# Overlap columns of the input-gradient tile copied by ScalarE in two instructions instead of four by GpSimd, its zeros written by VectorE, and the whole order planned anew

## The chip, the cores and the metric

The kernel runs on one core of a Trainium2 chip. It is timed in microseconds of the device, for one execution; the time of a kernel is the median of its runs. The core has five engines that each work through a list of their own: TensorE (PE in the profile; its weight loads are shown as PEld), VectorE (DVE), ScalarE (ACT), GpSimd (POOL) and SyncE (SP), which here does nothing but issue DMA transfers.

## What is computed

A 1-D convolution along time with 31 taps and stride 2, from 256 to 256 channels, then a normalisation of each channel over time, a scale and a shift, and the tanh form of GELU; and the gradients of all of it.

```python
B, T, D, K, s = 2, 16000, 256, 31, 2
L = (T - K) // s + 1                       # 7985
h = sum(jnp.einsum('blc,cd->bld', x[:, i:i + s*L:s, :], w[i]) for i in range(K))
mu  = jnp.einsum('bld->bd', h)[:, None, :] / L
var = jnp.einsum('bld->bd', (h - mu) ** 2)[:, None, :] / L
h = (h - mu) / jnp.sqrt(var + 1e-5)
out = gelu(h * gn_gamma + gn_beta)         # tanh form
# returned: out, and by vjp with grad_out: dx, dw, dgamma, dbeta
```

x has the shape (2, 16000, 256) and w (31, 256, 256), all in bfloat16. dx (the input gradient, out_1) is again a convolution, of the gradient before the normalisation with the taps in reverse; dw (out_2) is a sum over time for each tap.

## The kernel before, in words

**Stages.** The program runs forward (stages F0 and F1, matmuls on L814 that write 128x256), input gradient (G0 and G1, matmuls on L1369 that write 128x512) and weight gradient (W, matmuls on L1659 that write 128x256), for batch 0 and batch 1. The input gradient of batch 0 runs while the element work of batch 1 (GELU and its derivative) is done on DVE and ACT. Time is cut into four chunks c of each batch b, with 256 columns each (`HM`).

**Fewer multiplications.** The convolutions are done with a two-level splitting: of two parts of the taps and two parts of the data, three products are formed (branches `A`, `B_` and `C_`, with sums of the parts as operands), and within each branch once more. So each matmul group needs sums formed ahead of it by DVE, and joins of its results behind it by ACT and DVE.

**Input gradient, one chunk.** The gradient ahead of the normalisation is assembled in the tile `EG` by `e_comp` (L1260, L1263 and the addition `e_add`, L1251, all on DVE). `e_spread` then brings it into `ET`, a tile with two halves of channels, four phases k, two parities j and `EM` = 260 columns, by six ACT copies per chunk (`spread`, L1305; chunk (0,0) has none, its additions write into `ET` directly). Columns 2 to 257 of `ET` are the chunk's own; columns 0 and 1 are the last two of the chunk before, since the taps reach back. For chunk 0 they are zeros (`zero`, L618: memsets on POOL); for the chunks 1 to 3 they are copied inside `ET`, from columns 256 and 257, by four POOL copies (`cp`, L1296: two of 128x12 elements, one of 128x4, one of 128x2). These copies must wait until the sums of the chunk before (`g_sums`, L1332 on DVE) and the `B_` matmuls of the chunk before, which read `ET` directly, are done with it; and the ACT copies of `spread` must wait until the overlap is taken, since they write over columns 256 and 257. Six chunks have such an overlap: (0,1), (0,2), (0,3), (1,1), (1,2) and (1,3). In the last chunk of each batch `e_comp` also sets the columns of `EG` past the end to zero, by four memsets.

From `ET`, `g_sums` (L1332) builds the operands, the matmuls (L1369) run into one of four PSUM tiles (`ps_114` to `ps_117`, each 2 x 512 floats), and ACT empties these: `keep` (L868) copies a PSUM tile of 128x1024 to SBUF or to another PSUM tile, L1396 writes a negated copy of one half into the other half. `g_join` (L1411, DVE) adds the results of the branches into one of two output tiles, and `g_store` sends them to out_1. The two output tiles alternate: a `keep` that writes into one waits until that tile's last store has landed. `d2_piece` (L1555, DVE) prepares, between these, differences that the weight gradient reads back later, stored to `d2d`. `dn_turn` (L614) transposes `EG` by DMA and stores it to `dnd`.

**Order.** The order of the work is not written out by hand. Every operation is recorded with `Plan.add`: engine, an estimate of its duration, what it writes and what it reads. A list scheduler then plays the program through on a model of the five engines and the DMA queue, and at each step takes, among the operations that are ready on an engine, the one with the earliest due time. The due time is computed back from the operation's successors and shifted by a number from a table, `lead`, that has one entry per kind of operation (stage, helper, caller). Three passes are made, and `emit` pins the resulting order. Each engine then works through its list strictly in order, and nearly all transfers are issued from SP, in one list. So a number in the table moves operations in the lists of all engines, and a different engine for one operation moves others too.

Of the kernel before, what the change touches and what calls it, by code (L numbers as in the profile page):

```python
# [12 lines left out]
ACT = mybir.ActivationFunctionType  # L13
# [25 lines left out]
class Plan:  # L39
# [3 lines left out]
    def __init__(self, tc):  # L43
# [11 lines left out]
            "F0 conv_stem_kernel wrapper": 109.4,  # L55
            "F0 f_evac last": -1.7,
            "F0 f_join f_evac": 2.6,
            "F0 f_join split": 3.7,
            "F0 f_mm f_three_ac": -0.5,
            "F0 f_mm f_three_b": 0.7,  # L60
            "F0 f_three_b split": -75.0,
            "F0 keep f_evac": 5.3,
            "F0 keep split": -9.5,
            "F0 load conv_stem_kernel": 43.4,
            "F0 load f_evac": 2.8,
            "F0 load put": 0.4,
            "F0 load x_pre": 4.0,
            "F0 load_gb conv_stem_kernel": -22.9,
            "F0 tt f_sums": -3.6,
            "F0 tt second": 5.1,  # L70
            "F0 tt third": -3.4,
            "F0 turn w2_part": 1.2,
            "F0 turn x_load": -6.2,
            "F0 w_sub w2_part": -1.6,
            "F0 x_pre conv_stem_kernel": -0.1,
            "F0 zero conv_stem_kernel": 30.6,
            "F0 zero f_evac": -6.0,
            "F0 zero w2_part": -47.0,
            "F0 zero x_load": -17.6,
            "F0a f_evac last": 8.9,  # L80
            "F0a f_join f_evac": -2.0,
            "F0a f_join split": -16.3,
            "F0a f_mm f_leaf": -12.0,
            "F0a f_mm f_three_b": -24.3,
            "F0a f_mm pe_turn": 7.0,
            "F0a f_three_b f_first": 6.4,
            "F0a f_three_b split": -2.1,
            "F0a keep f_first": -23.9,
            "F0a keep split": -2.3,
            "F0a load load_w": 15.6,  # L90
            "F0a load x_load": 13.2,
            "F0a put x_first": -3.4,
            "F0a tt f_sums": -2.8,
            "F0a tt second": -0.3,
            "F0a tt third": -2.7,
            "F0a turn x_load": -35.7,
            "F0a ve f_first": -3.4,
            "F0a w_sub f_first": -2.1,
            "F0a zero load_w": -15.4,
            "F1 f_evac last": 3.7,  # L100
            "F1 f_join f_evac": 10.3,
            "F1 f_mm f_leaf": 0.3,
            "F1 f_mm f_three_ac": -0.5,
            "F1 f_three_b plain": 1.4,
            "F1 f_three_b split": 4.0,
            "F1 gelu_batch conv_stem_kernel": -1.5,
            "F1 gelu_unit gelu_batch": 1.0,
            "F1 keep f_evac": -3.0,
            "F1 keep plain": -4.8,
            "F1 keep split": -31.2,  # L110
            "F1 load f_evac": -10.0,
            "F1 load gelu_unit": 2.4,
            "F1 load out0_store": -4.3,
            "F1 tiny elem_finalize": -10.6,
            "F1 tiny fwd_stats": 2.8,
            "F1 tt f_sums": -6.5,
            "F1 tt second": 1.2,
            "F1 tt third": 0.4,
            "F1 turn gelu_batch": -2.1,
            "F1 turn gelu_unit": 5.9,  # L120
            "F1 turn x_load": 1.3,
            "F1 zero gelu_batch": -17.4,
            "F1z f_evac last": -0.7,
            "F1z f_join f_evac": -4.8,
            "F1z f_join split": 0.1,
            "F1z f_mm f_leaf": -0.9,
            "F1z f_mm f_three_ac": 0.6,
            "F1z f_mm f_three_b": -0.3,
            "F1z f_three_b split": -25.4,
            "F1z keep f_evac": -22.3,  # L130
            "F1z keep split": 0.1,
            "F1z load f_evac": 0.7,
            "F1z tt f_sums": -8.5,
            "F1z tt second": -3.7,
            "F1z tt third": 3.1,
            "F1z turn x_load": 9.7,
            "F1z w_sub f_again": -0.8,
            "F1z zero f_evac": -3.4,
            "F1z zero x_load": 19.3,
            "G0 cp e_spread": -23.3,  # L140
            "G0 e_add e_comp": -0.8,
# [1794 lines left out]
```

## Time and profile before

| | |
|---|---|
| three runs | 1122.73, 1120.94, 1117.76 us |
| their median | 1120.94 us |
| the profiled execution | 1115.62 us, its span 1113.8 us |
| mean granted TensorE clock | 0.998 of full speed |
| busy: PE, PEld | 1080.7, 795.8 us |
| busy: DVE, ACT, POOL | 997.6, 605.8, 37.4 us |
| L1296, the POOL copies | 24 instructions, 25.3 us busy |
| L1305, the ACT copies of `spread` | 42 instructions; idle before them ended by the POOL copies: 7.1 us in 3 places |

The profile is of one execution of its own, which ran 5.3 us below the median. Its span goes from the first to the last instruction on the core; 1.8 us of the execution lie around it. Busy times are what the hardware profiler saw on each engine. "Idle before" of a group of instructions is the time in which its engine had nothing running ahead of one of them, put down to whatever ended last of the things it waited for. In the rows of the timeline the columns are: start, busy time, engine, source line, operation, output <- input by the names of the program's buffers, size, count, and in brackets the idle time before the first and what ended it.

### The profile page before, as it was taken

What the parts mean: (1) busy time and instruction counts of PE and PEld (TensorE: products, weight loads), DVE (VectorE), ACT (ScalarE), POOL (GpSimd) and SP (SyncE); (2) the same over time, 40 slices, a digit from 0 to 9 for tenths busy, and PEclk for the clock granted to TensorE, in tenths of its full rate; (3) what the DMA queues carried; (4) which work ended last, traced back from release to release, by engine and by line L of the source; (5) the groups of instructions that cost most, each with busy time, mean ns of one, the idle gap of its engine ahead of it and who ended that gap; (6) DMA issues with size and microseconds to landing.
All of it is one profiled execution on the core that took longest, in us unless ns stands there. A gap on an engine that the chain in (4) does not pass through costs nothing. (4 is left out here: it accounts for less than half of the span.)

```text
span 1113.8 us, 19741 instructions
## 1 busy us (share of the span) xinstructions
PE 1080.7 (97%) x8094; PEld 795.8 (71%) x8132; DVE 997.6 (90%) x1039; ACT 605.8 (54%) x838; POOL 37.4 (3%) x67
## 2 busy tenths in 40 slices
PE   5999999999999999999999998999999999999998
PEld 4888899888888984444444443444468888888887
DVE  6995968789999996999899988889789999999996
ACT  1244444688788649797767566676643323332232
POOL 0000000000000010020200011000000000000000
PEclk9999999999999999999999999999999999999999
DMA  9369999995979699987675999988797655696974
GB/s 227 54 178 242 278 268 270 256 175 147 193 169 244 211 288 311 263 231 237 179 244 149 318 317 290 292 286 284 253 297 228 229 205 165 242 326 206 301 213 124
DMA packets 346894, 261.47 MB, mean 235 GB/s; under 512 B 187702, under 2 KB 315572, under 8 KB 340916
## 3 DMA queue, kind: packets, MB, share of 16 engines
q1 hardware_dynamic: 346612, 260.22, 82.4%
q8 instruction: 63, 1.03, 0.4%
q14 instruction: 27, 0.22, 0.1%
q0 software_dynamic: 192, 0.00, 0.0%
HBM read 120.00 MB, written 94.86 MB: 193 GB/s over the span
## 5 line engine op out<-in xcount | busy, mean ns | idle before, releaser
L814 PE MATMUL ps<-arena 128*128 128x256 bf16 (+3 forms) x3668 | 396.7, 271 | 17.0 <-DMA arena<-in_x_dram 7.7
L1369 PE MATMUL ps<-arena 128*128 128x512 bf16 (+1 forms) x1834 | 400.6, 377 | 8.9 <-ACT arena L868 4.2
L814 PEld LDWEIGHTS <-arena 128*128 128x128 bf16 x3668 | 359.0, 99 | 54.4 <-DMA arena<-in_x_dram 8.2
L1369 PEld LDWEIGHTS <-arena 128*128 128x128 bf16 x1872 | 183.6, 98 | 225.2 <-issue 11.7
L868 ACT ACTIVATE arena<-ps 128x1024 bf16<-128x1024 f32 (+1 forms) x187 | 190.0, 1022 | 240.5 <-PE ps L1659 118.5
L1659 PE MATMUL ps<-arena 128*128 128x256 bf16 x2592 | 284.0, 273 | 3.0 <-DVE arena L1613 2.3
L1659 PEld LDWEIGHTS <-arena 128*128 128x128 bf16 x2592 | 253.2, 98 | 34.0 <-DVE arena L1613 3.6
L782 DVE TENSOR_TENSOR arena<-arena 128x2064 bf16<-128x2064 bf16 (+5 forms) x132 | 164.1, 1266 | 26.6 <-PE ps L814 22.8
L1167 DVE TENSOR_TENSOR arena<-arena 128x2048 bf16<-128x2048 bf16 (+1 forms) x80 | 95.4, 1194 | 9.4 <-ACT arena L1159 4.4
L1332 DVE TENSOR_TENSOR arena<-arena 128x1032 bf16<-128x1032 bf16 (+7 forms) x111 | 86.0, 796 | 5.3 <-PE ps L1369 4.8
L1396 ACT ACTIVATE ps<-ps 128x512 f32<-128x512 f32 x108 | 62.8, 586 | 25.3 <-PE ps L1369 25.1
L1155 ACT ACTIVATE arena<-arena,stats 128x1024 bf16<-128x1024 bf16 (+1 forms) x64 | 74.5, 1207 | 1.3 <-DVE stats L1101 0.8
L1555 DVE TENSOR_TENSOR arena<-arena 128x1536 bf16<-128x1536 bf16 (+3 forms) x56 | 62.3, 1124 | 13.3 <-DMA d2d<-arena 12.2
L1622 DVE TENSOR_TENSOR arena<-arena 128x4096 bf16<-128x4096 bf16 x32 | 72.2, 2285 | 0.4 <-DMA arena<-in_x_dram 0.3
L844 ACT ACTIVATE ps<-ps 128x512 f32<-128x512 f32 x59 | 34.3, 582 | 70.2 <-PE ps L814 70.1
L1411 DVE TENSOR_TENSOR arena<-arena 128x1024 bf16<-128x1024 bf16 (+1 forms) x70 | 63.3, 914 | 9.4 <-ACT arena L868 9.0
L1731 ACT COPY ps<-ps 128x512 f32<-128x512 f32 x54 | 30.8, 571 | 64.7 <-PE ps L1659 64.7
L1718 DVE TENSOR_TENSOR arena<-arena 128x2048 bf16<-128x2048 bf16 x54 | 64.7, 1218 | 0.3 <-DMA arena<-d2d 0.3
L1613 DVE TENSOR_TENSOR arena<-arena 128x4096 bf16<-128x4096 bf16 (+1 forms) x32 | 62.1, 1952 | 0.1
L1665 DVE TENSOR_TENSOR arena<-arena 128x1024 bf16<-128x1024 bf16 x75 | 48.8, 684 | 7.8 <-ACT arena L868 7.7
L890 ACT ACTIVATE arena<-ps 128x512 bf16<-128x512 f32 (+1 forms) x64 | 36.7, 579 | 34.8 <-PE ps L814 34.5
L767 DVE TENSOR_TENSOR arena<-arena 128x2048 bf16<-128x2048 bf16 (+1 forms) x45 | 50.5, 1147 | 1.4 <-DMA vl<-arena 1.4
(72 smaller groups left out, 536.9 us busy)
## 6 DMA issues: line engine op xcount, KB each, us to landing
arena<-in_x_dram SPq DMA_DIRECT2D x28, 1024.0 KB, 9.6
arena<-d2d SPq DMA_DIRECT2D x16, 1216.0 KB, 7.4
out_dram<-arena SPq DMA_DIRECT2D x35, 512.0 KB, 4.1
d2d<-arena SPq DMA_DIRECT2D x30, 384.0 KB, 5.6
arena<-dnd SPq DMA_DIRECT2D x10, 960.0 KB, 6.2
arena<-vl SPq DMA_DIRECT2D x9, 1024.0 KB, 8.7
hd<-arena SPq DMA_DIRECT2D x8, 1024.0 KB, 6.8
arena<-in_x_dram SPq DMA_DIRECT2D x32, 256.0 KB, 4.9
```

The source lines that it names most:

```text
L782: lambda: nc.vector.tensor_tensor(out=o, in0=a, in1=b, op=ALU.add))
L814: yield nc.tensor.matmul(ps[:, dh, cs], lhsT=wt, rhs=mv, start=s0, stop=False, skip_group_check=True)
L868: lambda: nc.scalar.activation(out=out, in_=ps, func=ACT.Copy, scale=scale))
L1155: lambda o=o, func=func, i=h[:, dh], sc=sc, bi=bi: SC.activation(out=o, in_=i, func=func, bias=bi, scale=sc))
L1167: add("DVE", dve(8 * wd), [o], [a, b_], lambda: V.tensor_tensor(out=o, in0=a, in1=b_, op=op))
L1332: lambda: nc.vector.tensor_tensor(out=o, in0=a, in1=b, op=ALU.add))
L1369: yield nc.tensor.matmul(ps[:, e, 0:wide], lhsT=lt, rhs=mv, start=s0, stop=False, skip_group_check=True)
L1396: lambda: nc.scalar.activation(out=ps[:, 1], in_=ps[:, 0], func=ACT.Copy, scale=-1.0))
L1411: add("DVE", dve(o.free_size(), rate), [o], [a, b], lambda: nc.vector.tensor_tensor(out=o, in0=a, in1=b, op=op))
L1622: add("DVE", dve(4096), [o], [a, b], lambda: nc.vector.tensor_tensor(out=o, in0=a, in1=b, op=ALU.add))
L1659: yield nc.tensor.matmul(ps[:, s, c0:c1], lhsT=lt, rhs=mv, start=s0, stop=False, skip_group_check=True)
L1718: add("DVE", dve(2048), [d4], [d], lambda: nc.vector.tensor_tensor(out=d4, in0=fan(d[:, o0:o0 + 3 * s + 1:s, :], 1, (o1 - o0) * D), in1=fa ...
```

## The change

`e_spread` takes the overlap with two ACT copies in place of four POOL copies, by seeing the four phases and two parities of `ET` as one dimension of eight: the first copy has 2 x 7 x 2 = 28 elements per partition, the second 2. The zeros of chunk 0 become two DVE memsets (28 and 2 elements) in place of four on POOL, and the zeros past the end of `EG` two DVE memsets (50 and 364 elements) in place of four on POOL. Per execution 24 POOL copies and 16 POOL memsets go, 12 ACT copies and 8 DVE memsets come. The table `lead` has new numbers in nearly all of its entries (225 in place of 224), so that the lists of all engines change from one end of the program to the other; the matmuls and the transfers are the same in number and size.

```diff
         self.lead = {
-            "F0 conv_stem_kernel wrapper": 109.4,
+            "F0 conv_stem_kernel wrapper": 128.0,
...
-            "G1 cp e_spread": 2.0,
+            "G1 e_spread conv_stem_kernel": 0.5,
...
         if c == 3:
-            zero(EG[:, :, 0, 0, 231:HM], 50)
-            zero(EG[:, :, 0, 1:4, 230:HM], 156)
-            zero(EG[:, 0, 1, :, 230:HM], 104)
-            zero(EG[:, 1, 1, :, 230:HM], 104)
+            v = EG.rearrange("p d e k f -> p d (e k) f")
+            zero(v[:, :, 0, 231:HM], 50, "DVE")
+            zero(v[:, :, 1:8, 230:HM], 364, "DVE")

     def e_spread(b, c):
         et = ET
+        ev = et.rearrange("p d k j f -> p d (k j) f")
         if c == 0:
-            for dh in range(2):
-                zero(et[:, dh, 0:3, :, 0:2], 12)
-            zero(et[:, :, 3, 0, 0:2], 4)
-            zero(et[:, :, 3, 1, 0:1], 2)
+            zero(ev[:, :, 0:7, 0:2], 28, "DVE")
+            zero(ev[:, :, 7, 0:1], 2, "DVE")
         else:
-            def cp(o, i):
-                add("POOL", 0.3, [o], [i], lambda: nc.gpsimd.tensor_copy(out=o, in_=i))
-            for dh in range(2):
-                cp(et[:, dh, 0:3, :, 0:2], et[:, dh, 0:3, :, 256:258])
-            cp(et[:, :, 3, 0, 0:2], et[:, :, 3, 0, 256:258])
-            cp(et[:, :, 3, 1, 0:1], et[:, :, 3, 1, 256:257])
+            for o, i in ((ev[:, :, 0:7, 0:2], ev[:, :, 0:7, 256:258]), (ev[:, :, 7, 0:1], ev[:, :, 7, 256:257])):
+                add("ACT", act(o.free_size()), [o], [i], lambda o=o, i=i: nc.scalar.copy(out=o, in_=i))
```

What the new order does is seen in the lists of the engines. Below, `arena` is the one SBUF buffer that holds nearly all tiles, `ps0_114` and so on are the four PSUM tiles, and line numbers of the kernel after are one higher up to `e_comp` and five lower behind `e_spread`: `keep` is L869 there, the transposes L615, the loads and stores L610, `spread` L1300, the negated copy L1391, and the new copies are L1295.

First place, ACT, where chunk (0,3) of the input gradient begins (in the trace of before from 539 us). Before:

```order
L868 ACTIVATE arena_110<-ps0_114 128x1024
L1396 ACTIVATE ps1_115<-ps1_115 128x512
L1305 COPY arena_110<-arena_110 128x3x256
L1180 ACTIVATE arena_110,esum1_108<-arena_110 128x1024
L868 ACTIVATE arena_110<-ps3_117 128x1024
L1180 ACTIVATE arena_110,esum1_108<-arena_110 128x1024
L1155 ACTIVATE arena_110<-arena_110,stats_101 128x4x232 x2
L868 ACTIVATE ps0_114<-ps1_115 128x1024
L1396 ACTIVATE ps3_117<-ps3_117 128x512
```

After, at the same place:

```order
L869 ACTIVATE arena_110<-ps0_114 128x1024
L1295 COPY arena_110<-arena_110 128x2x7x2
L1295 COPY arena_110<-arena_110 128x2
L869 ACTIVATE arena_110<-ps3_117 128x1024
L1181 ACTIVATE arena_110,esum1_108<-arena_110 128x1024
L1391 ACTIVATE ps1_115<-ps1_115 128x512
L1181 ACTIVATE arena_110,esum1_108<-arena_110 128x1024
L1156 ACTIVATE arena_110<-arena_110,stats_101 128x4x232 x2
L1391 ACTIVATE ps3_117<-ps3_117 128x512
L869 ACTIVATE ps0_114<-ps1_115 128x1024
L869 ACTIVATE arena_110<-ps2_116 128x1024
L1300 COPY arena_110<-arena_110 128x3x256
```

The two overlap copies stand between two `keep`s, the `keep` of `ps3_117` has moved ahead of the first `spread` copy and of the element work, and the first `spread` copy has moved to the end of this stretch, behind the operations that empty PSUM.

Second place, ACT, at the spread of chunk (1,2) (in the trace of before from 676 us). Before:

```order
L868 ACTIVATE arena_110<-ps3_117 128x1024
L1305 COPY arena_110<-arena_110 128x3x256
L868 ACTIVATE arena_110<-ps1_115 128x2x512
L1305 COPY arena_110<-arena_110 128x3x256
L1396 ACTIVATE ps2_116<-ps2_116 128x512
L868 ACTIVATE arena_110<-ps0_114 128x1024
```

After:

```order
L869 ACTIVATE arena_110<-ps2_116 128x2x512
L1295 COPY arena_110<-arena_110 128x2x7x2
L1300 COPY arena_110<-arena_110 128x3x256
L1391 ACTIVATE ps2_116<-ps2_116 128x512
L1300 COPY arena_110<-arena_110 128x3x256
L1391 ACTIVATE ps3_117<-ps3_117 128x512
L869 ACTIVATE arena_110<-ps1_115 128x2x512
L869 ACTIVATE arena_110<-ps0_114 128x1024
L1391 ACTIVATE ps1_115<-ps1_115 128x512
L1295 COPY arena_110<-arena_110 128x2
L1300 COPY arena_110<-arena_110 128x3x256
```

The large overlap copy stands right ahead of the first `spread` copy, and the small one eight rows further on, ahead of the `spread` copy that writes over its two columns.

Third place, SP, while the output tiles of chunk (1,1) are filled; out_1 is the store of an output tile, the transposes are those of `EG` of chunk (1,2). Before (in the trace from 643 to 656 us, and from 663 us):

```order
L609 DMA out_1_dram<-arena_110 416x1x512
L609 DMA arena_110<-dnd0_80 128x3840
L609 DMA d2d0_86<-arena_110 128x3x256 x2
L609 DMA dnd1_81<-arena_110 1024x1x256 x2
L609 DMA d2d0_86<-arena_110 128x2x768
L609 DMA arena_110<-dyd1_2_74 128x4096
L609 DMA d2d0_86<-arena_110 128x2x768
```

```order
L609 DMA out_1_dram<-arena_110 512x1x512
L609 DMA d2d0_86<-arena_110 128x2x768
L609 DMA out_1_dram<-arena_110 512x1x512
L614 DMA_TRANSPOSE arena_110<-arena_110 128x16x128 x2
L609 DMA d2d0_86<-arena_110 128x2x768 x2
```

After, in one piece:

```order
L610 DMA arena_110<-dyd1_2_74 128x4096
L610 DMA d2d0_86<-arena_110 128x2x768
L610 DMA out_1_dram<-arena_110 416x1x512
L610 DMA arena_110<-hd1_2_66 128x4096
L610 DMA d2d0_86<-arena_110 128x3x256 x2
L610 DMA d2d0_86<-arena_110 128x2x768
L610 DMA arena_110<-dnd0_80 128x3840
L610 DMA out_1_dram<-arena_110 512x1x512
L610 DMA d2d0_86<-arena_110 128x2x768
L615 DMA_TRANSPOSE arena_110<-arena_110 128x16x128 x2
L610 DMA out_1_dram<-arena_110 512x1x512
L610 DMA d2d0_86<-arena_110 128x2x768 x2
```

The store of 416 rows has moved past eight transfers, to behind the load of `dyd1_2`, and the last of the three stores from ahead of the two transposes to behind them.

More of the change, by code (lines that the diff above doesn't have):

```diff
@@ L127, in __init__ @@
+            "F1z f_join split": 12.8,
+            "F1z f_mm f_leaf": -1.8,
             "F1z f_mm f_three_ac": 0.6,
             "F1z f_mm f_three_b": -0.3,
[L129 to L135, printed above, removed]
+            "F1z f_three_b split": -28.4,
+            "F1z keep f_evac": -35.4,
@@ L270, in __init__ @@
-            "Wz w_mm w_single": -43.1,
-            "Wz w_pairs weight_grad": -43.9,
-            "Wz w_sum w_done": -22.2,
+            "G1z keep last": 6.8,
+            "G1z keep split": 4.1,
+            "G1z load g_store": 1.9,
+            "G1z tt first": 12.1,
+            "G1z tt outer": 12.3,
+            "G1z tt second": -30.0,
+            "G1z tt third": -3.1,
+            "W keep w_done": -2.7,
+            "W keep weight_grad": -5.8,
+            "W leaf_d weight_grad": -0.2,
+            "W load d_tile": -5.5,
```

338 lines of the change are left out of this document (167 added, 171 removed).

## The prediction

> **What bounds the kernel now.** I read the page's first part, then the waits by engine, then the timeline round the places where the overlap columns are copied.
>
> ```profile
> span 1113.8 us, 19741 instructions
> PE 1080.7 (97%) x8094; PEld 795.8 (71%) x8132; DVE 997.6 (90%) x1039; ACT 605.8 (54%) x838; POOL 37.4 (3%) x67
> ```
>
> PE is the bound: it stands still for 1113.8 - 1080.7 = 33.1 us only, and the change leaves the matmuls as they are. So the whole question is which of these 33.1 us move. DVE has 116 us of idle time, ACT 508.
>
> ```profile
> PE ps L814 <- DMA arena<-in_x_dram: 7.7, 3, 4.5
> PE ps L814 <- DVE arena L767: 5.8, 1, 5.8
> PE ps L1369 <- ACT arena L868: 4.2, 3, 2.7
> PE ps L1659 <- DVE arena L1613: 2.3, 2, 1.2
> PE ps L1369 <- ACT ps L868: 1.5, 2, 1.3
> PE ps L1369 <- ACT ps L1396: 1.2, 4, 0.4
> PE ps L814 <- ACT ps L868: 1.0, 1, 1.0
> PE ps L814 <- ACT arena L890: 1.0, 1, 1.0
> PE ps L814 <- DVE arena L782: 0.8, 2, 0.6
> PE ps L1659 <- ACT arena L868: 0.7, 2, 0.4
> PE ps L814 <- ACT ps L844: 0.7, 1, 0.7
> ACT arena L1305 <- POOL arena L1296: 7.1, 3, 3.8
> ```
>
> These are PE's waits (total us, times, longest) and the one ACT wait on the POOL copies. The first two rows, 13.5 us, are the start of the program: the first loads and operand sums, before any matmul. The other nine sum to 13.4 us; those are the stalls inside the program, and no order of the work can win more than them. POOL stops ACT three times, 7.1 us in all; PE never waits for POOL itself. What the change can win is therefore what PE waits for ACT behind those three.
>
> **The copies.**
>
> ```profile
> L1296 POOL COPY arena<-arena 128x12 bf16<-128x12 bf16 (+2 forms) x24 | 25.3, 1096 | 172.3 <-DVE arena L1332 165.3 <-PE ps L1369 7.0
> L1305 ACT COPY arena<-arena 128x768 bf16<-128x768 bf16 x28 | 22.5, 827 | 7.8 <-POOL arena L1296 7.1 <-DVE arena L1251 0.7
> L1305 ACT COPY arena<-arena 128x512 bf16<-128x512 bf16 x14 | 8.4, 617 | 0.3
> L1830 DVE MEMSET arena<- 128x512 uint32 x1 | 0.5, 485 | 0.1
> ```
>
> POOL spends 25.3 us on 24 copies, 4.2 us for each of the six groups. The price of an ACT copy of this size is not in the trace. The nearest rows are ACT's own SBUF copies: 827 ns for 768 elements, 617 for 512, so (827 - 617) / 256 = 0.82 ns for an element and 617 - 0.82 x 484 = 220 ns for 28. I take 0.22 us each. The lower end is nothing (if it overlaps its neighbours wholly), the upper end is POOL's own 1.10 us, should it be the pieces of two elements that cost. All 12 then take 2.6 us of ACT (0 to 13) in 508 us of its idle time. The eight DVE memsets are bounded by nothing and 0.485 us each, so 0 to 3.9 us; the largest has 364 elements against the row's 1024 of the same width, and I take 1 us in all. It lies in DVE's 116 us of idle time; without that cover it would be 1 us on PE. The 16 POOL memsets that go stand in none of PE's waits above, so they give nothing.
>
> The 1.10 us of the POOL copies is odd for 12 elements. The Trainium skill, "SBUF — State Buffer", section "Who interferes with whom", has a reason: a DVE instruction with two SBUF inputs and a GpSimd instruction that reads SBUF contend for a shared port, and the later one waits until the other has ended, while ScalarE has ports of its own. DVE's additions in the timeline below (L1332 and others) are of this kind, but no run here separates a blocked port from a slow engine or a costly shape. By that rule the ACT copies need no upper end of 1.10 us, and the sum below stands; if instead the shape costs, a group takes 2.2 us on ACT, the stalls of 1.30 and 0.25 us below stay, and the sum is about 0 (-1.7 + 1.3 + 0.2), the time of the last rival.
>
> **First place: chunk (0,3).**
>
> ```profile
> 541.89 5.18 POOL L1296 COPY arena<-arena 128x12 bf16<-128x12 bf16 x4 [3.13 <-DVE arena L1332]
> ...
> 544.73 0.83 ACT L1305 COPY arena<-arena 128x768 bf16<-128x768 bf16 x1 [3.79 <-POOL arena L1296]
> ...
> 546.51 1.00 ACT L868 ACTIVATE arena<-ps 128x1024 bf16<-128x1024 f32 x1
> ...
> 547.57 2.75 PE L1369 MATMUL ps<-arena 128*128 128x512 bf16 x12 [0.42 <-ACT arena L868]
> ...
> 550.56 1.00 ACT L868 ACTIVATE ps<-ps 128x1024 f32<-128x1024 f32 x1
> ...
> 551.61 4.70 PE L1369 MATMUL ps<-arena 128*128 128x512 bf16 x21 [1.30 <-ACT ps L868]
> ```
>
> DVE's sums release the copies at 541.89; ACT stands until 544.73, and its list is late from there on. PE waits for the `keep` of 546.51 (0.42 us) and for that of 550.56 (1.30 us). In the new order the two copies come next in ACT's list; released by the same sums at 541.9 they end at 542.3, and the `keep` of `ps3_117` runs directly behind them, 3 us earlier than before. The second `keep` has the element work of L1181 and L1156 ahead of it as before, but no `spread` copy and no 3.79 us of waiting, so it is earlier too. Both stalls go: -0.42 - 1.30 = -1.7 us. What is late next is the `spread`, which moves to the end of that stretch; its readers are the DVE sums of the next chunk, a unit away. If the sums (L1332) are placed later on DVE, the copies now hold ACT's list, with both PSUM `keep`s behind them, where before they held only POOL's: this is the new wait of the change, and it can give the 1.7 back.
>
> **Chunk (1,1).**
>
> ```profile
> 642.46 0.83 ACT L1305 COPY arena<-arena 128x768 bf16<-128x768 bf16 x1 [1.12 <-POOL arena L1296]
> 650.28 19.59 PE L1369 MATMUL ps<-arena 128*128 128x512 bf16 x90 [0.25 <-ACT ps L1396]
> ```
>
> ACT loses 1.12 us and works without a pause up to a negated copy that PE waits 0.25 us for. With 0.44 us of copies in place of the 1.12, it goes: -0.2 us.
>
> **Second and third place: chunk (1,2) and the stores of the output tiles.**
>
> ```profile
> 643.29 0.94 SPq L609 DMA_DIRECT2D out_dram<-arena  x1
> 654.82 0.41 SPq L609 DMA_DIRECT2D arena<-dyd  x1
> 669.83 0.54 SPq L609 DMA_DIRECT2D out_dram<-arena  x1
> 670.97 5.44 SPq L614 DMA_TRANSPOSE arena<-arena  x2
> ```
> ```profile
> 661.49 1.02 ACT L868 ACTIVATE arena<-ps 128x1024 bf16<-128x1024 f32 x1 [1.08 <-PE ps L1369]
> 671.48 1.02 ACT L868 ACTIVATE arena<-ps 128x1024 bf16<-128x1024 f32 x1 [5.25 <-DMA out_dram<-arena]
> 672.55 10.31 PE L1369 MATMUL ps<-arena 128*128 128x512 bf16 x39 [2.68 <-ACT arena L868]
> 677.20 4.13 POOL L1296 COPY arena<-arena 128x12 bf16<-128x12 bf16 x4 [32.42 <-DVE arena L1332]
> 680.03 0.83 ACT L1305 COPY arena<-arena 128x768 bf16<-128x768 bf16 x1 [2.21 <-POOL arena L1296]
> 680.77 1.02 ACT L868 ACTIVATE arena<-ps 128x1024 bf16<-128x1024 f32 x1
> 682.92 1.01 ACT L868 ACTIVATE arena<-ps 128x1024 bf16<-128x1024 f32 x1
> 683.99 6.20 PE L1369 MATMUL ps<-arena 128*128 128x512 bf16 x27 [1.12 <-ACT arena L868]
> ```
> ```profile
> out_dram<-arena SPq DMA_DIRECT2D x6, 512.0 KB, 8.0
> ```
>
> The last row is from the DMA view between 600 and 700 us: a store lands 8.0 us after its issue. Here ACT waits 2.21 us for POOL, and PE 1.12 us for the `keep` of 682.92. The large copy now stands alone ahead of the first `spread`, so this stall goes: -1.1 us. The small copy is the one that waits for the `B_` matmuls; it stands behind two more `keep`s, and only one `spread` copy directly behind it needs it.
>
> What is late next is the output tile. The `keep` of 671.48 shows the price: it waited 5.25 us for a store to land and PE lost 2.68, so ACT has 2.57 us of slack there. I leave this stall as it is, since its store has kept its place. The `keep` of 680.77 writes the other tile, whose store left at 669.83; behind the transposes it leaves at 670.97 + 5.44 = 676.4 and lands at 684.4. With the copies, two `spread` copies and two negated copies ahead of it, that `keep` could again start at about 680.8: ACT waits 3.6 us and PE loses 3.6 - 2.57 = 1.0. Lower end 0 (a store that lands in 5.6 us), upper end 2.7 as at 671.48. The store of 643.29 moves to behind the load of 654.82 and another transfer, to about 655.5, and lands at 663.5 against a `keep` that started at 661.49: 2.0 us, inside the slack, so 0, with the same upper end of 2.7.
>
> **The sum.** -1.7 - 0.2 - 1.1 + 1.0 = -2.0; the copies of the other three groups, (0,1), (0,2) and (1,3), add 0.44 us to ACT each where POOL delayed nothing, 0 to 1.3 on PE, and I take 0.3. Sum -1.7 us. The other 10.3 us of stalls inside the program (13.4 - 0.42 - 1.30 - 0.25 - 1.12, the 2.68 among them) are left in kind: the new order will move them, with a sign that no row tells. Against the profiled execution (1115.62 us, of which 1.8 lie outside the span) that gives 1113.9. That execution is 5.3 us under the median of the three runs, so the median becomes 1120.94 - 1.7 = 1119.2 us. A measurement can tell about 0.5%, 5.6 us, from no change; the forecast is inside this.
>
> **The rivals.**
>
> *The new order removes much of the other stalls.* For it: every list is rearranged, and there is 10.3 us to win. Against it: the stalls are small and come from four causes on three engines. If the first output store too comes early enough for the 2.68 to go, and half of the remaining 7.6, it is -1.7 - 2.7 - 3.8 = -8.2: 1112.7 us.
>
> *The output tiles come free late.* For it: two of three stores in a row are moved behind other transfers on SP, 6 and 12 us later, and the 2.68 us stall, the largest inside the program, is already of this kind; ACT's list holds PSUM copies behind such a `keep`. Against it: before, ACT waited for a store only once. It decides from the point where a store lands over 2.57 us after its `keep` could start; each us past this is one on PE. With a stall of 2.68 at the two moved stores and at two more of the later chunks, 4 x 2.68 = 10.7 instead of the 1.0 in the sum: -1.7 - 1.0 + 10.7 = +8.0, 1128.9 us, slower than before.
>
> *The gain is hidden.* The copies may wait in ACT's list for DVE's sums as long as POOL kept ACT waiting: then both stalls of the first place stay, and the sum is 0: 1120.9 us.
>
> **How the numbers follow.** The forecast has a chance of 0.33, its own range is 1115 to 1125: with the copies and the two stores at their ends the sum runs from -3.0 to +3.7, so 1117.9 to 1124.6, and I leave 3 us below for stalls that the new order takes away unseen. The first rival has 0.32, the second 0.23, the third 0.12. The range goes from 1110 (10.9 us of the 13.4 gone) to the second rival's 1129. Faster by over 0.5% is the first rival, 0.32; slower is the second, 0.23; within are the forecast and the third, 0.45.
>
> **What would show it right or wrong.** In the profile after: POOL's busy time at 12 us or less (37.4 - 25.3), no wait of ACT on POOL copies; L1295 with 12 copies of 0.2 us, not 1; no PE stall over 0.3 us within 15 us of the first overlap copy of chunk (0,3); PE waits of 1 us or less behind a `keep` that waits for out_1. The prediction is wrong if ACT waits for DVE's sums ahead of L1295 for 3 us or more, if ACT waits for out_1 at several places, or if the sum of PE's stalls inside the program falls under 8 us or rises over 19.

## The result, and the profile after

The kernel after runs in 1114.69 us (median of 12 runs), the kernel before in 1121.54 us (12 runs beside them); the ratio is 0.9943, with a 95% interval from 0.9923 to 0.9963. That is 6.4 us less (4.1 to 8.6), where 1.7 us less was forecast. Over all executions of this study the means are 1119.84 us (107 of the kernel before) and 1113.76 us (31 of the kernel after): 6.1 us. Two executions, one of each of two kernels of the experiments, took 2321 and 2953 us and are left out of the ratios and means.

The two profiled executions don't show this. The one of before was near the fastest of its kernel and the one of after near the slowest of its own; their spans are 1113.8 and 1114.8 us. So nothing can be read from the difference of the two totals; single places can.

The first part of the page of after:

```profile
span 1114.8 us, 19701 instructions
PE 1080.4 (97%) x8094; PEld 795.4 (71%) x8132; DVE 998.6 (90%) x1047; ACT 607.1 (54%) x850; POOL 10.4 (1%) x27
```

PE's waits in it:

```profile
PE ps L815 <- DMA arena<-in_x_dram: 8.3, 4, 7.0
PE ps L815 <- DVE arena L768: 5.8, 1, 5.8
PE ps L1654 <- DVE arena L1608: 4.5, 6, 1.4
PE ps L1364 <- ACT arena L869: 2.7, 2, 2.2
PE ps L815 <- ACT ps L845: 1.9, 1, 1.9
PE ps L815 <- ACT ps L869: 1.5, 1, 1.5
PE ps L1654 <- ACT arena L869: 1.1, 1, 1.1
PE ps L1364 <- ACT ps L1391: 1.0, 2, 0.6
```

PE's waits for ACT in the input gradient (L1364) have fallen from 6.9 to 3.7 us. The stalls inside the forward (L815, without the start) and the weight gradient (L1654) are together 3.9 us larger than in the profile of before, which hides the gain in this execution. A second profile of the unchanged kernel before, taken later, has 5.3 us of stalls in the weight gradient and 6.2 in the forward, where the first had 2.9 and 3.4: these stages vary that much from one execution to the next.

The new copies, grouped by shape (busy, mean ns of one):

```profile
L1295 ACT COPY arena<-arena 128x28 bf16<-128x28 bf16 x6 | 1.3, 212 | 2.0 <-DVE arena L1327 1.9
L1295 ACT COPY arena<-arena 128x2 bf16<-128x2 bf16 x6 | 1.2, 192 | 0.0
```

The three places of the prediction, in the timeline of after; first chunk (0,3), on ACT and then on PE:

```profile
542.78 0.32 ACT L1295 COPY arena<-arena 128x28 bf16<-128x28 bf16 x2 [1.35 <-DVE arena L1327]
543.91 1.02 ACT L869 ACTIVATE arena<-ps 128x1024 bf16<-128x1024 f32 x1 [0.82 <-PE ps L1364]
```
```profile
438.31 195.07 PE L1364 MATMUL ps<-arena 128*128 128x512 bf16 x898 [0.42 <-ACT ps L1391]
```

Both copies of the group take 0.32 us where POOL took 5.18. From 438 to 633 us PE has no stall that the timeline separates: the 0.42 and 1.30 us are gone. Then chunks (1,1) and (1,2) with the stores of the output tiles:

```profile
653.35 0.94 SPq L610 DMA_DIRECT2D out_dram<-arena  x1
662.27 1.94 ACT L869 ACTIVATE arena<-ps 128x1024 bf16<-128x1024 f32 x2 [2.47 <-DMA out_dram<-arena]
664.26 5.34 PE L1364 MATMUL ps<-arena 128*128 128x512 bf16 x24 [0.56 <-ACT arena L869]
670.72 1.02 ACT L869 ACTIVATE arena<-ps 128x1024 bf16<-128x1024 f32 x1 [4.75 <-DMA out_dram<-arena]
671.79 149.06 PE L1364 MATMUL ps<-arena 128*128 128x512 bf16 x674 [2.19 <-ACT arena L869]
674.06 0.99 SPq L610 DMA_DIRECT2D out_dram<-arena  x1
677.80 0.22 ACT L1295 COPY arena<-arena 128x28 bf16<-128x28 bf16 x1 [0.52 <-DVE arena L1327]
681.07 1.94 ACT L869 ACTIVATE arena<-ps 128x1024 bf16<-128x1024 f32 x2
```

The stalls of 0.25 and 1.12 us are gone too. The store of 653.35, moved behind eight transfers, makes a `keep` wait 2.47 us and PE 0.56; the store of 674.06, moved behind the transposes, makes nobody wait (the `keep` of 681.07 starts without idle time); the stall of 2.68 us is now 2.19. In two further profiles of the kernel after the first of these waits is 2.00 and 1.56 us and PE loses nothing behind it, and the stall near 672 us is 3.45 and 2.24 us.

### The profile page after: what moved, and what is told of

Read it like the earlier page. It is cut to its first block, busy times and chain, and to the rows that moved or that the text cites. A ratio compares the mean times of both kernels' runs of the same rounds, so it can differ in the third digit from the quotient of the medians.

```text
span 1114.8 us, 19701 instructions
## 1 busy us (share of the span) xinstructions
PE 1080.4 (97%) x8094; PEld 795.4 (71%) x8132; DVE 998.6 (90%) x1047; ACT 607.1 (54%) x850; POOL 10.4 (1%) x27
## 5 line engine op out<-in xcount | busy, mean ns | idle before, releaser
L815 PE MATMUL ps<-arena 128*128 128x256 bf16 (+3 forms) x3668 | 396.4, 271 | 18.5 <-DMA arena<-in_x_dram 8.3
L1364 PE MATMUL ps<-arena 128*128 128x512 bf16 (+1 forms) x1834 | 400.2, 378 | 6.1 <-ACT arena L869 2.7
L815 PEld LDWEIGHTS <-arena 128*128 128x128 bf16 x3668 | 358.9, 99 | 55.8 <-DMA arena<-in_x_dram 8.6
L1364 PEld LDWEIGHTS <-arena 128*128 128x128 bf16 x1872 | 183.6, 98 | 222.1 <-issue 7.4
L869 ACT ACTIVATE arena<-ps 128x1024 bf16<-128x1024 f32 (+1 forms) x187 | 189.4, 1022 | 239.5 <-PE ps L1654 120.7
L1654 PE MATMUL ps<-arena 128*128 128x256 bf16 x2592 | 284.4, 273 | 5.6 <-DVE arena L1608 4.5
L1654 PEld LDWEIGHTS <-arena 128*128 128x128 bf16 x2592 | 253.0, 98 | 37.0 <-DVE arena L1608 7.5
L783 DVE TENSOR_TENSOR arena<-arena 128x2064 bf16<-128x2064 bf16 (+6 forms) x132 | 164.1, 1268 | 27.4 <-PE ps L815 23.8
L1327 DVE TENSOR_TENSOR arena<-arena 128x1036 bf16<-128x1036 bf16 (+6 forms) x111 | 86.4, 798 | 9.1 <-PE ps L1364 8.9
L1391 ACT ACTIVATE ps<-ps 128x512 f32<-128x512 f32 x108 | 63.0, 586 | 29.6 <-PE ps L1364 29.2
L891 ACT ACTIVATE arena<-ps 128x512 bf16<-128x512 f32 (+1 forms) x64 | 36.7, 578 | 34.3 <-PE ps L815 34.3
```

Source lines behind the costliest of these rows:

```text
L783: lambda: nc.vector.tensor_tensor(out=o, in0=a, in1=b, op=ALU.add))
L815: yield nc.tensor.matmul(ps[:, dh, cs], lhsT=wt, rhs=mv, start=s0, stop=False, skip_group_check=True)
L869: lambda: nc.scalar.activation(out=out, in_=ps, func=ACT.Copy, scale=scale))
L1327: lambda: nc.vector.tensor_tensor(out=o, in0=a, in1=b, op=ALU.add))
L1364: yield nc.tensor.matmul(ps[:, e, 0:wide], lhsT=lt, rhs=mv, start=s0, stop=False, skip_group_check=True)
L1654: yield nc.tensor.matmul(ps[:, s, c0:c1], lhsT=lt, rhs=mv, start=s0, stop=False, skip_group_check=True)
```

## The experiments

The length of the input gradient, from the start of its first matmul to that of its last, is read from the view of the PSUM tiles, and the sum of the idle times ahead of its PE rows from the timeline. Two or three profiles of one kernel are listed side by side. Every ratio is to the kernel before on the same chip; the experiments ran on three chips, on which the kernel before has means of 1118.8 to 1120.3 us, so medians of different rows compare less well than ratios. Lines that a kernel adds shift its line numbers, so L876 or L891 below is `keep`, L1398 the negated copy, L1297 or L1304 the POOL copy.

| kernel | copies by | median us | ratio to before, 95% interval | input gradient, us | PE's stalls in it, us |
|---|---|---|---|---|---|
| before | POOL | 1119.8 (107 executions) | | 409.6, 408.7, 410.2 | 6.9, 6.3, 8.6 |
| after | ACT | 1114.0 (31 executions) | 0.9943 [0.9923, 0.9963] | 406.3, 406.8, 404.5 | 4.1, 4.8, 3.6 |
| old order | ACT, four a group | 1115.0 | 0.9952 [0.9932, 0.9972] | 406.0, 403.8 | 5.1, 2.8 |
| old order, POOL copies beside | ACT, four a group | 1115.5 | 0.9971 [0.9951, 0.999] | 405.2 | 4.3 |
| old order, three chunks with a stall | ACT there, else POOL | 1117.0 | 0.9971 [0.9953, 0.9989] | 407.4 | 4.0 |
| old order, the other three | ACT there, else POOL | 1120.8 | 1.0003 [0.9985, 1.002] | 412.4 | 9.5 |
| new order | POOL, two a group | 1116.9 | 0.9977 [0.9951, 1.0003] | 411.7 | 9.4 |
| new order, store first | ACT | 1112.9 | 0.9955 [0.9936, 0.9973] | 404.9 | 3.7 |
| the same, copy later | ACT | 1113.1 | 0.993 [0.9905, 0.9956] | 404.6 | 3.7 |

**The old order with ACT copies.** Theory A: the engine of the copies makes the difference. Theory B: the new order does.

```diff
-                add("POOL", 0.3, [o], [i], lambda: nc.gpsimd.tensor_copy(out=o, in_=i))
+                add("POOL", 0.3, [o], [i], lambda: nc.scalar.copy(out=o, in_=i))
```

The planner still places the copy as POOL work, so no other row of any engine's list moves.

> The order of the kernel before, kept row by row; only the 24 overlap copies are issued by ScalarE where GpSimd issued them, still four to a group. If the copies' engine makes the difference (theory A), the three stalls of PE behind the waits on POOL go, 1.72 us at chunk (0,3), 0.25 us at (1,1), 1.12 us at (1,2), and the time falls by about 3 us or more, to 1118 us or below. If the new order makes it (theory B), this kernel stays within 2 us of the kernel before, at 1120 to 1122 us, and most of the 6.4 us is seen only with the new order. If the four copies hold ACT's list while they wait for DVE's sums, the stalls come back in part and the gain is 1 us or none.

> The old order with ScalarE copies once more, for a second profile: the input gradient takes 406.6 us within 0.6 us, with no stall at chunk (0,3). If the weight gradient is again at 287 us and that of the kernel before at 290 us, the copies also move something there; if it lies between, the difference is between executions.

It ran at 1115.0 us, 0.9952 of the kernel before, and the second profile at 1111.1 us. PE's rows between 440 and 707 us:

```profile
440.34 208.84 PE L1369 MATMUL ps<-arena 128*128 128x256 bf16 x961 [0.18 <-ACT ps L868]
649.42 19.59 PE L1369 MATMUL ps<-arena 128*128 128x512 bf16 x90 [0.24 <-ACT ps L1396]
671.60 33.70 PE L1369 MATMUL ps<-arena 128*128 128x512 bf16 x153 [2.59 <-ACT arena L868]
706.24 113.92 PE L1369 MATMUL ps<-arena 128*128 128x512 bf16 x521 [0.94 <-ACT arena L868]
```

The stalls of chunk (0,3) and the 1.12 us at (1,2) are gone without any new order; the 0.25 us at (1,1) stayed in this profile and is absent in the second. Theory A holds: this kernel and the kernel after differ by 0.4 us in their means (1114.17 of 13 executions, 1113.76 of 31), which is less than the 0.7 us that their scatter leaves uncertain. Since the zeros are still POOL's here, they too are worth nothing that can be measured. The gain, 5 us, was larger than the 3 us that theory A gave in numbers.

**The new order with POOL copies.**

```diff
-                add("ACT", act(o.free_size()), [o], [i], lambda o=o, i=i: nc.scalar.copy(out=o, in_=i))
+                add("ACT", act(o.free_size()), [o], [i], lambda o=o, i=i: nc.gpsimd.tensor_copy(out=o, in_=i))
```

> The order of the kernel after, kept row by row, with the zeros on DVE; only the 12 overlap copies (28 and 2 elements) are issued by GpSimd. Theory A: the copies again take 2 to 5 us a group on POOL, ACT's spread copies wait for them in the same three places, and the time is 3 us or more above the kernel after, 1118 us or more. Theory B: the new order alone keeps the gain, 1114 to 1117 us.

It ran at 1116.9 us, which lies in the range of theory B (1114 to 1117) and not in that of theory A (1118 or more); its interval reaches from 5.5 us faster than the kernel before to no difference. Its mean is 3.1 us above that of the kernel after on the same chip (1117.41, 1114.30; uncertain by 1.2), as theory A has it. So this kernel alone decides little; the old order with ACT copies decides. The twelve copies took 17.6 us on POOL, against 25.3 for the 24 of before, and ACT waited for them at two places, chunks (1,1) and (1,2), not at three. POOL's row at chunk (1,2), ACT's behind it and PE's behind that:

```profile
677.67 5.98 POOL L1295 COPY arena<-arena 128x28 bf16<-128x28 bf16 x2 [40.38 <-DVE arena L1327]
683.56 0.83 ACT L1300 COPY arena<-arena 128x768 bf16<-128x768 bf16 x1 [7.89 <-POOL arena L1295]
684.93 141.29 PE L1364 MATMUL ps<-arena 128*128 128x512 bf16 x639 [5.14 <-ACT ps L1391]
```

A stall of 5.14 us at this place is larger than anything the copies cost in the profiles of before. So what a POOL group costs varies from one order to another.

**The two kernels again.** 

> The kernel before, unchanged, timed against itself and profiled once more. Its times should show a ratio of 1 within 0.3%. The profiled execution of before ran at 1115.6 us, near the lowest of its 12 timed ones (1115.3 to 1124.7): if a typical execution loses 5 to 6 us that this one did not lose, the stalls of PE inside the program or at its start are larger in the new profile by that amount and stand in one place; theory C says that this place is a DMA wait (the first loads, or a keep that waits for a store to out_1), and that the new order is faster because it waits there less. If the new profile has the same stalls at a time of about 1121 us, the difference lies in the duration of the matmuls or outside the span.

> The kernel after, unchanged: ratio 0.994 +- 0.002 to the kernel before, 1112 to 1117 us. Its second profile has no PE stall over 0.3 us near the overlap copies of chunk (0,3), the same wait for out_1 with about 2.2 us on PE after 670 us, and, by theory C, start and store waits that differ less from the first profile than those of before do.

> The kernel before once more, for a third profile: if theory A holds, the input gradient (from the first matmul on L1369 to the first on L1659) takes 409 to 410 us as in the two profiles so far, against 406.5 to 407 us where ScalarE copies; the forward and the weight gradient vary by 2 to 4 us from one execution to the next, in both kernels.

> The kernel after, unchanged, beside the three others on the same chip: 1112 to 1116 us, ratio 0.995 within 0.002 to the kernel before; its input gradient takes 406.5 to 407.5 us with a wait of 2.2 to 3.5 us near 672 us.

The kernel before against itself gave 1.0002 [0.9982, 1.0022]; the two further series of the kernel after gave 1113.85 us, 0.9952 [0.9931, 0.9972], and 1110.95 us, 0.9931 [0.9905, 0.9957]. Theory C (the missing microseconds stand in one DMA wait) falls: the second profile of before is 6.8 us longer than the first, of which 0.8 us is the start, 3.0 the forward and 3.9 the weight gradient, while the input gradient is 0.9 shorter; in the two longer stages the stalls stand in six and three places, and no one of them is over 2.4 us. In the input gradient itself the three profiles of before lie at 408.7 to 410.2 us and the three of after at 404.5 to 406.8: 3.6 us less in the mean. The other stages are not shorter in the profiles of after: the input gradient begins at 412.7 to 416.5 us before and at 414.2 to 414.8 after, and the weight gradient takes 291.1 to 295.0 us before and 292.6 to 294.1 after. Part of the rest goes with PE's clock: over the executions of this case whose clock is on record the granted clock lies between 0.992 and 1.000, a line through them, with the mean of each kernel taken out, gives 1.08 us for each 0.001, and the kernel before averages 0.9977 (95 executions) where the kernel after averages 0.9984. That is 0.7 us. Some 1.8 us of the 6.1 are not placed.

**POOL busy beside ACT's copies.** Is it the wait, or the work of POOL itself?

```diff
-                add("POOL", 0.3, [o], [i], lambda: nc.scalar.copy(out=o, in_=i))
+                def both():
+                    yield nc.scalar.copy(out=o, in_=i)
+                    n = o.free_size()
+                    ...
+                    yield nc.gpsimd.tensor_copy(out=w, in_=v)
+                add("POOL", 0.3, [o], [i], both)
```

Here v is a piece of `EG` of the same size and w a scratch tile of 128x32 elements.

> The old order with ScalarE copies, as in the experiment before, and beside each of them a GpSimd copy of the same size that reads the tile EG and writes a scratch tile nobody reads. POOL is as busy as in the kernel before, about 25 us, at nearly the same places, but no ScalarE copy waits for it. Theory A1 (the wait of the spread copies for POOL is the whole cost): the time stays at that of the old order with ScalarE copies, 1113 to 1117 us, with the same stalls of PE in the input gradient, about 5.4 us. Theory A2 (POOL's work itself costs, by blocking VectorE's second read port or by lowering the granted clock): the time goes back by 2 us or more, to 1117 to 1120 us, and VectorE's busy time rises or the granted clock is under 0.998 in more executions than the one in six seen with ScalarE copies.

It ran at 1115.5 us, in the range of theory A1. POOL's group in it:

```profile
L1304 POOL COPY scr<-arena 128x12 bf16<-128x12 bf16 (+2 forms) x24 | 63.0, 2625 | 113.7 <-DVE arena L1264 66.5 <-DVE arena L1252 46.0
```

POOL was busy for 63.0 us with these copies, two and a half times as long as in the kernel before, DVE's busy time was 997.5 us as before (997.6), and the input gradient took 405.2 us. The length of the input gradient is that of the kernels with ACT copies alone. The mean is 1.0 us above that of the same kernel without them (1115.20, 1114.17), each uncertain by about 0.6, but that one ran on another chip; by the ratios the difference is 2 us (0.9971, 0.9952), with intervals that overlap. So nothing of POOL's work by itself is seen in DVE or in the input gradient, where the wait for it costs 3.6 us; in the total a cost of 1 to 2 us is not excluded.

**Three chunks at a time.**

```diff
+                copy = nc.scalar.copy if (b, c) in ((0, 3), (1, 1), (1, 2)) else nc.gpsimd.tensor_copy
-                add("POOL", 0.3, [o], [i], lambda: nc.gpsimd.tensor_copy(out=o, in_=i))
+                add("POOL", 0.3, [o], [i], lambda: copy(out=o, in_=i))
```

The other kernel has the chunks (0,1), (0,2) and (1,3) in the list.

> The old order; only the copies of the three chunks at which ACT waited for POOL, (0,3), (1,1) and (1,2), are issued by ScalarE, those of (0,1), (0,2) and (1,3) stay on GpSimd. If the three waits are the whole cost (theory A1), the time falls as far as with all copies on ScalarE, to about 1114 to 1115 us, and the input gradient takes 405 to 407 us. If the copies also cost where no wait was seen (theory A3), only a part of the 5.6 us comes, 1116 to 1118 us.

> The counterpart: ScalarE copies only at (0,1), (0,2) and (1,3), where the profile of before shows no wait of ACT for POOL; the other three stay on GpSimd. Theory A1: no gain, 1118.5 to 1121 us as the kernel before, the input gradient at 409 to 410.5 us, with the stalls of 0.42 and 1.30 us at chunk (0,3). Theory A3: 2 to 3 us faster than the kernel before.

The three chunks at which ACT waited for POOL give 3 us (0.9971), the other three nothing (1.0003). The first kernel's 1117.0 us lies in the range of theory A3 (1116 to 1118) and not in that of theory A1 (1114 to 1115), its input gradient of 407.4 us just past A1's 407; the second kernel's 1120.8 us lies in A1's range, and A3's 2 to 3 us for the other three chunks were not found. So the waits seen in the profile carry what can be seen of the effect; whether they carry all of it is open, since the first figure's distance from the 5 us of all six is within the intervals (0.9953 to 0.9989 against 0.9932 to 0.9972). At chunk (1,1) POOL's group takes 2.85 us in all three profiles of before; in the first of them:

```profile
641.92 2.85 POOL L1296 COPY arena<-arena 128x12 bf16<-128x12 bf16 x4 [37.89 <-DVE arena L1332]
```

In the second kernel the same group looks like this; POOL, ACT and PE:

```profile
644.47 8.04 POOL L1297 COPY arena<-arena 128x12 bf16<-128x12 bf16 x4 [36.74 <-DVE arena L1333]
652.15 0.83 ACT L1306 COPY arena<-arena 128x768 bf16<-128x768 bf16 x1 [7.12 <-POOL arena L1297]
653.51 36.05 PE L1370 MATMUL ps<-arena 128*128 128x512 bf16 x160 [6.09 <-ACT ps L1397]
```

The view of this one line gives the durations of its 12 copies, shortest, median and longest in ns:

```profile
L1297 POOL COPY arena<-arena x12: 185/667/7647, 545.5 to 686.9; 128x12 bf16<-128x12 bf16 x6, 128x4 bf16<-128x4 bf16 x3, 128x2 bf16<-128x2 bf16 x3
```

And DVE beside it, from the release of the copies to their end:

```profile
643.62 1.90 DVE L1333 TENSOR_TENSOR arena<-arena 128x1032 bf16<-128x1032 bf16 x3
645.45 1.21 DVE L1412 TENSOR_TENSOR arena<-arena 128x2048 bf16<-128x2048 bf16 x1
646.59 2.44 DVE L1333 TENSOR_TENSOR arena<-arena 128x1032 bf16<-128x1032 bf16 x3
...
651.29 0.68 DVE L1333 TENSOR_TENSOR arena<-arena 128x1032 bf16<-128x1032 bf16 x1
651.90 0.14 DVE L1226 TENSOR_TENSOR small<-stats,small 128x2 f32<-128x2 f32 x1
```

One copy of 12 elements lasted from 644.47 to 652.1 us. DVE ran operations on two SBUF tiles (`TENSOR_TENSOR`) without a gap from 643.62 to 652.0; when they ended, the copy ended, and the other three took 0.45 us together.

**The store first, and the copy later.** What is left near 671 us is the wait for the store of an output tile. In the first kernel SP issues this store ahead of the 983 KB load that stood before it (and one like it in batch 1); in the second, ACT's list at chunk (1,2) also has the overlap copy and two `spread` copies behind the two negated copies that followed.

```diff
+        for a, b in zip(sp, sp[1:]):
+            if self.ops[a]["kind"] == "G1 load d2_piece" and self.ops[a]["dma"] > 2.0 and self.ops[b]["kind"].endswith("load g_store"):
+                p, q = seq.index(a), seq.index(b)
+                if not any(a in self.ops[j]["preds"] for j in seq[p + 1:q + 1]):
+                    seq.insert(q, seq.pop(p))
```

> The kernel after, in which SP issues the first store of an output tile of chunk (1,1) ahead of the 983 KB load it stood behind (and likewise once in batch 1, chunk (1,2) or (1,3)); nothing else moves. If the wait for out_1 near 670 us is the price of an output tile that comes free late, as the prediction had it, the store leaves 2.2 us earlier and lands at least that much earlier, ACT's wait of 4.75 us falls to 2.6 us or less, the PE stall behind it (2.2 to 3.5 us) to under 0.5 us, and the time by about 2 us, to 1111 to 1113 us. If the landing is set by the load on the DMA rings anyway or PE's win is given back to VectorE later, the stall goes and the time stays at 1114 us; if the delayed load makes VectorE's differences late, a new stall of 1 us or more stands in its place.

It ran at 1112.9 us; its mean is 0.3 us below that of all executions of the kernel after (1113.47, 1113.76), which is no difference. In its timeline:

```profile
666.96 1.02 ACT L876 ACTIVATE arena<-ps 128x1024 bf16<-128x1024 f32 x1 [2.82 <-DMA out_dram<-arena]
...
676.21 0.22 ACT L1302 COPY arena<-arena 128x28 bf16<-128x28 bf16 x1 [4.37 <-DVE arena L1334]
...
677.83 1.02 PE L1371 MATMUL ps<-arena 128*128 128x512 bf16 x4 [1.87 <-ACT ps L1398]
```

ACT's wait for the store fell from 4.75 to 2.82 us, and PE's stall behind it from 2.19 to 0.26. But ten microseconds later the overlap copy holds ACT for 4.37 us, because DVE's sums are not done, and PE loses 1.87 us at a negated copy behind it. This is the wait that the prediction named, for chunk (0,3), as the new one of the change.

The second kernel moves that copy:

```diff
+        seg = act_[j:j + 8]
+        neg = [i for i in seg if "g_three_b" in self.ops[i]["kind"]][:2]
+        move = [i for i in seg[:seg.index(neg[-1])] if i not in neg]
...
+            seq = rest[:q] + move + rest[q:]
```

> The kernel with the store issued first, in which ACT's list at chunk (1,2) has the overlap copy and the first two spread copies behind the two negated copies that stood after them. There ACT waited 4.37 us for VectorE's sums with these negated copies behind it, and PE lost 1.87 us. If the new wait is as the prediction named it (the copy holds PSUM work in ACT's list until DVE's sums are done), that stall goes and the time falls by 1 to 2 us, to 1111 to 1112 us; if VectorE is simply late there, the stall moves to the next keep, of which the next matmuls wait, and the time stays at 1113 to 1114 us.

It ran at 1113.1 us, as forecast for the case that VectorE is simply late, and the kernel after beside it at 1110.95. The copy now waits 0.37 us only. PE loses 0.97 us at a `keep` that stands 13 us ahead of the copy and waits 2.89 us for a store, and 1.20 us at a `keep` right behind the copy:

```profile
664.01 14.84 PE L1386 MATMUL ps<-arena 128*128 128x512 bf16 x68 [0.97 <-ACT arena L891]
680.04 24.12 PE L1386 MATMUL ps<-arena 128*128 128x512 bf16 x112 [1.20 <-ACT arena L891]
```

So the stall removed first came back ten microseconds later, and the one removed next came back in part behind the moved copy; the stalls in the input gradient stayed at 3.7 us, against 3.6 to 4.8 in the kernel after. Counted from the first matmul of the input gradient, the overlap copy of chunk (1,2) starts at 263.2 to 264.5 us in the three profiles of the kernel after and at 263.6 and 264.0 us in these two, each time released by VectorE's sums. What sets the pace of this stretch is then VectorE, and moves on SP and ACT shift only where PE loses the time; this is read from the traces, no run tests it. No version was found that is measurably faster than the kernel after.

## Why the prediction was right, and where its size was off

The direction and the range held (1114.7 us in 1110 to 1129), but the range of 19 us reaches over both rivals, and the result lies 0.3 us below the forecast's own range of 1115 to 1125. The forecast of -1.7 us was between a quarter and a third of what was measured, and the result lies 0.07% past the bound of 0.5% that was taken for no change: it falls where the prediction put its first rival. So the mechanism was right where it could be followed in the trace, and that the stated range holds the time is in part luck. Of the signs that were named, POOL's busy time (10.4 us), the price of the copies, the absence of waits for POOL and the clean stretch at chunk (0,3) came; PE's wait of 1 us or less behind a `keep` that waits for out_1 did not (2.19 us, where the sum itself had left 2.68), and ACT waits for out_1 at two places where it did at one.

*The three stalls.* The terms -1.7, -0.2 and -1.1 came as worked out: all three are absent after the change, and the old order with ACT copies shows that those of chunks (0,3) and (1,2) go with the engine alone.

*The price of the copies.* 0.22 us each was taken, 0.21 and 0.19 were measured. The upper end of 1.10 us, should the shape of the pieces cost, is excluded. The eight DVE memsets took 0.9 us together, against the 1 us taken, and cost nothing on PE that shows.

*The charges, +1.0 and +0.3.* This is the first mis-sized term. The second store did leave after the transposes, at 674.06, but nobody waited for it; the `keep` started at 681.07 as forecast, and the store had landed by then: a landing of 8.0 us, a median over one stretch of before, was too long for it. The price came at the other moved store, forecast as 2.0 us inside ACT's slack of 2.57: 2.47 us of waiting, 0.56 on PE, and nothing on PE in the two other profiles. The copies of the other three chunks cost at most 0.2 us (a stall of 0.36 us at 434 us became 0.56). With these sizes the sum would have been -3.0 + 0.56 + 0.2 = -2.2 us.

*What POOL cost before.* This is the second mis-sized term: the three waits were priced as one execution showed them. The POOL groups take the same times in all three profiles of before, to 0.01 us, but ACT stood 7.1, 5.3 and 9.7 us behind them; the rows of the second and third:

```profile
ACT arena L1305 <- POOL arena L1296: 5.3, 2, 3.8
ACT arena L1305 <- POOL arena L1296: 9.7, 3, 3.8
```

PE's stalls that follow sum to 3.1, 2.2 and 5.7 us, 3.7 in the mean, where the sum has 3.0. The experiments also show groups of POOL copies of 8.0 and 6.0 us, with PE stalls of 6.1 and 5.1 us behind them, in kernels that mix the engines or the orders; whether such long ones occur in other executions of the kernel before, no profile shows. The measured input gradient became shorter by 3.6 us (4.6 in the two profiles of the old order with ACT copies), not by the 1.7 of the sum.

*The rest.* The other stalls were "left in kind", with no sign. That held for the new order: it is worth 0.4 us, within its uncertainty, so the first rival (the new order removes much) was wrong as a mechanism, though the time came near its figure of 1112.7. The second rival (output tiles late) was seen at two stores, at 2.75 us on PE together where the profile of before has 2.68, so it decided nothing. The base was a favourable one: PE's stalls inside the program, by the timeline, sum to 13.2 us in the profile from which the prediction worked, to 17.8 and 17.5 in the two later ones of before, and to 14.3, 13.6 and 12.5 in those of after. Of 6.1 us between the means, 3.6 are in the input gradient and 0.7 go with the granted clock; for the remaining 1.8 us the cause stays open, since forward and weight gradient vary by up to 4 us between executions of the same kernel. Whether the lower clock of the kernel before has to do with the copies stays open too. On each of the three chips the kernels in which ACT makes all copies have a higher mean clock than the kernel before (0.9983 and 0.9985 against 0.9973; 0.9985 and 0.9990 against 0.9981; 0.9984 and 0.9998 against 0.9982), and the three others with copies on POOL in the path do not (0.9968, 0.9973 and 0.9973), so the clock may belong to the gain. The kernel with POOL copies beside ACT's is among the higher ones (0.9985), which speaks against POOL's work as such.

*The rule on ports.* The prediction weighed what the Trainium skill, "SBUF — State Buffer", section "Who interferes with whom", says: a DVE instruction with two SBUF inputs and a GpSimd instruction that reads SBUF exclude each other, and ScalarE has ports of its own. This case's traces agree: 7.65 us for 12 elements under an unbroken run of DVE operations on two SBUF tiles, 0.45 us for three copies after its end, 0.21 us on ACT. They also show a copy held over some ten DVE instructions in a row, and a DVE that lost nothing.

## What to carry to other kernels

A tiny operation on GpSimd whose result another engine waits for was priced here by what VectorE did beside it, not by its size: if the engine that waits can do it itself in 0.2 us, it should, even at two more entries in its list. The cost of such a wait differs from one execution to the next, so take it from several profiles. A move that removes one stall of a tightly planned stretch should be followed for some 15 us downstream, since the next late engine can take it back.

## What the runs showed of the hardware that was not expected

A GpSimd copy of 12 elements for each partition took between 0.19 and 7.65 us, and one of 28 elements 5.85 us; these two long ones ended only as VectorE's run of two-input SBUF operations ended. In the kernel with POOL copies beside ACT's, one lasted 17.44 us, from 630.71 to 648.15, while VectorE ran such operations from one into the next. It is not always so: at chunk (1,1) three profiles of before show the group at 2.85 us beside the same VectorE rows, so a copy can also get through between two VectorE instructions; which one happens, the traces don't tell. VectorE paid nothing for it: 997.5 us busy with 63 us of such copies, 997.6 with 25.

A ScalarE copy in SBUF costs 192 ns for 2 elements and 212 ns for 28: nearly all of it is fixed.
